# Decode layer on one core: projection, gate and up with the matrix as the moving operand, rows turned by small matmuls, and 128 rows of w_down loaded as 121 and 7

## Chip, cores and metric

One NeuronCore of a Trainium2 chip runs the whole kernel, written in Bass with its waits placed by hand. The metric is the device time of one execution in microseconds (us); the median of three executions of the kernel before is 203.09 us.

## The reference

One token of a decoder layer with cached attention and a gated feed-forward part, all in bf16. There is one row of 640 numbers, 32 heads of 128, 4096 cached positions and 1728 hidden columns:

```python
B, Sq, D = 1, 1, 640
Hq, Hkv, Sk, Dh = 32, 32, 4096, 128
...
q = (x @ wq).reshape(B, Sq, Hq, Dh).transpose(0, 2, 1, 3)
scores = jnp.einsum("bhqd,bhkd->bhqk", q, k) * (Dh ** -0.5)
p = _softmax(scores, axis=-1)
o = jnp.einsum("bhqk,bhkd->bhqd", p, v)
return o.transpose(0, 2, 1, 3).reshape(B, Sq, Hq * Dh) @ wo
...
g = jnp.einsum("bsd,df->bsf", x, w_gate)      # 640 x 1728
u = jnp.einsum("bsd,df->bsf", x, w_up)
h = _gelu(g) * u
return jnp.einsum("bsf,fd->bsd", h, w_down)   # 1728 x 640
...
x = A_x
h = x + _A_ref(_layernorm(x), A_k_cache, A_v_cache, A_wq, A_wo)
h2 = h + _B_ref(_layernorm(h), B_w_gate, B_w_up, B_w_down)
```

The matrices are read once each: the caches are 32 MB each, wq and wo 5 MB each, the three matrices of the feed-forward part 2.2 MB each.

## The kernel before

**Queues.** Every operation is put into a list of its engine by the helpers `V` (VectorE), `A` (ScalarE), `T` (TensorE), `GP` (GpSimd) and `P.dma`. `emit` writes the lists out engine by engine in the order in which they were filled, and `_run` puts a semaphore wait ahead of an operation for what it depends on. All large loads are issued from SyncE's queue (SP) in a fixed order; the issue of a load into a slot waits for the work that frees that slot. The helper `matmul_again` (line 28) is a matmul that uses the weights that are already loaded.

**Attention.** The heads go in eight groups `G` of four. `order` is K0 V0 K1 V1 ... K5 V5 K6 K7 V6 V7; each is a 4 MB load into one of three slots. For a group of K, `score_mult` (L287) multiplies on VectorE, `fold` sums on TensorE, and `score_exp` reduces (L305) and exponentiates (L309) into `p_bd`. For a group of V, `pv_group` multiplies on TensorE with four column tiles side by side into `po`, two PSUM banks. `pick` (L345) keeps the rows that belong together, `pick_sum` (L350) adds them into `po_r`, `p_sum` (L341) sums the exponentials, and `head_sum` (L356) puts the group's heads into place. `scores` runs what `first` and `later` hold, so that the sums of one group are queued among the multiplications of the next.

**Projection.** After four groups `z_sum`, `normalize`, `spread` and `take` leave the heads' output as the columns `aP`. `proj_part` (L386) uses w_o as the stationary operand: each of its 160 matmuls for one half loads a strided 128x128 block and moves one column, so the 640 sums come out as five columns over the partitions, `ps_p`. w_o is loaded in three pieces, `d_wo["0"]`, `["1a"]` and `["1b"]`, into the arena that held wq.

**Feed-forward part.** `h` (L463) adds the input, `layernorm` makes `hlnT`, and `hX` and `resid` (L485) put the residual into the result's bank `ps_d`. `glu` (L476) uses w_gate and then w_up as the stationary operand, 70 matmuls of one column each, into the 14 columns of `ps_g` and `ps_u`. Column m holds the hidden numbers in the order in which w_down's rows lie on the partitions. Operations g1 to g9 (L491 to L499) make `hm`. `down` moves w_down, 160 columns at a time into four column tiles (L506), and four copies and one DMA write the result. The rows 1536 to 1663 of w_down (`wd_sb[:, 12, :]`, 1,280 bytes each) are one load, the first that SP issues after the last V group's matmuls; then come the rows 1664 to 1727, w_gate, w_up in two pieces and the rest of w_down in four pieces.

Of the kernel before, what the change touches and what calls it, by code (L numbers as in the profile page):

```python
# [6 lines left out]
BF16 = mybir.dt.bfloat16  # L7
ALU = mybir.AluOpType
ACTF = mybir.ActivationFunctionType
AX = mybir.AxisListType  # L10

D = 640
# [3 lines left out]
DF = 1728  # L16
# [4 lines left out]
NG = 8  # L21
# [88 lines left out]
def bass_sequential_preLN__gqa_block_cached__glu_gated_geglu__decode_kernel(nc, A_x, A_k_cache, A_v_cache, A_wq, A_wo, B_x, B_w_gate, B_w_up, B_w_down, out):  # L110
# [25 lines left out]
    aP = sb("aP", [128, 2, 16], BF16)  # L136
    sel = sb("sel", [16, 8, 128], BF16)
    g_t = sb("g_t", [128, 14], FP32)
    t1 = sb("t1", [128, 14], FP32)
# [52 lines left out]
    def issue(upto):  # L192
        while state["next"] < min(upto, len(order)):
# [8 lines left out]
                         for i in range(parts)]  # L202
# [20 lines left out]
                                        pattern=[[-1, 4], [-4, 32]], compare_op=ALU.is_equal,  # L223
                                        fill=0.0, base=0, channel_multiplier=1), c_ones)
    c_m8 = GP(lambda e: e.affine_select(m8_t[:, :, :, :], ones_f[:, :].rearrange("p (a b c) -> p a b c", a=8, b=4),
                                        pattern=[[-4, 8], [-32, 4], [-1, 4]], compare_op=ALU.is_equal,
# [8 lines left out]

    c_hs = V(lambda e: e.reduce_sum(hs[:, 12:16], hs_t[:, :, :], axis=AX.X), c_hs, c_hz)
    c_m8 = V(lambda e: e.reduce_sum(m8[:, :], m8_t[:, :, :, :].rearrange("p a b c -> p a (b c)"), axis=AX.X), c_m8)

# [109 lines left out]

    def pick_sum(G):
        evs[G] = V(lambda e: e.reduce_sum(po_r[:, G % 2, :], po_m[:, :, :].rearrange("p b d -> p d b"), axis=AX.X),  # L350
                   mks[G], hds.get(G - 2))
# [30 lines left out]
    def proj_part(t, lo, hi, *ws):  # L382
        def fn(e):
            for c in range(5):
                for i in range(lo, hi):
                    r = e.matmul(ps_p[:, c:c + 1], wo_sb[:, t, i, c::5], aP[:, t, i:i + 1],  # L386
                                 start=(t == 0 and c == 0 and i == 0), stop=(t == 1 and i == 15),
                                 skip_group_check=True)
            return r
        return T(fn, *ws)  # L390
# [3 lines left out]
    def run(todo):  # L394
        while todo:
            todo.pop(0)()

    def scores(G):
        for i in range(4):
            score_mult(4 * G + i)  # L400
            if i >= 1:
                score_exp(4 * G + i - 1)
        run(first)
        score_exp(4 * G + 3)
        run(later)
        issue(pos[("K", G)] + 1 + NSLOT)

    headed = 0
    for kind, G in order:
# [9 lines left out]
        first.append(lambda G=G: pick(G))  # L419
        later += [lambda G=G: pick_sum(G), lambda G=G: p_sum(G)]  # L420
        if G == 4:
            z_sum(0)
            later.append(lambda: normalize(0))
        if G == 5:
# [16 lines left out]
    wd_d = wd_sb[:, 0:12, :].rearrange("p (a r) n -> p a r n", a=3)  # L441
    d_wd = [P.dma("sync", wd_sb[:, 12, :], B_w_down[1536:1664, :], free[1]),
            P.dma("sync", wd_sb[:, 13, 0:320], B_w_down[1664:1728, :].rearrange("f (s n) -> (f s) n", s=2))]
# [5 lines left out]

    V(lambda e: e.memset(ps_g[64:128, 13:14], 0.0), reds[31])  # L450
    V(lambda e: e.memset(ps_u[64:128, 13:14], 0.0), reds[31])
    p_sum(NG - 1)
    pick(NG - 1)
    pick_sum(NG - 1)
    proj_part(0, 0, 16, aPs[0], d_wo["0"])
    z_sum(1)
# [4 lines left out]
    proj_part(1, 0, 12, aPs[1], d_wo["1a"])  # L461
    pr = proj_part(1, 12, 16, d_wo["1b"])
    h = V(lambda e: e.tensor_add(hT[:, 0:5], xx[:, 0:5], ps_p[:, 0:5]), pr)  # L463
    hl = layernorm(hT, h, lambda e: e.tensor_scalar(  # L464
        hlnT[:, :], hT[:, 0:5], ln[:, 0:1], ln[:, 4:5], ALU.subtract, ALU.mult))
# [3 lines left out]

    def glu(ps, w, cs):  # L470
        def fn(e):
            for c in cs:
                for m in range(14):
                    ws = w[:, c, 512 * (m // 4) + m % 4:512 * (m // 4) + 512:4] if m < 12 else \
                        w[:, c, 128 * m:min(128 * m + 128, DF)]
                    i = e.matmul(ps[0:128 if m < 13 else 64, m:m + 1], ws, hlnT[:, c:c + 1],  # L476
                                 start=(c == 0 and m == 0), stop=(c == 4), skip_group_check=True)
            return i
        return fn
    ga = T(glu(ps_g, wg_sb, range(5)), hl, d_wg)  # L480


    def resid(e):
        for q in range(4):
            i = e.matmul(ps_d[32 * q:32 * q + 1, 0:160], ones_f[:, 0:1],  # L485
                         hX[:, 32 * q:32 * q + 32, :].rearrange("p a c -> p (a c)"), start=True, stop=False)
        return i
    T(resid, hx)
    T(glu(ps_u, wu_sb, range(3)), d_wu[0])
    up = T(glu(ps_u, wu_sb, range(3, 5)), d_wu[1])  # L490
    g1 = V(lambda e: e.tensor_copy(g_t[:, :], ps_g[:, 0:14]), ga)  # L491
# [5 lines left out]
    g8 = V(lambda e: e.reciprocal(t1[:, :], t2[:, :]), g7)  # L497
    g6 = V(lambda e: e.tensor_mul(gu[:, :], g_t[:, :], t1[:, :]), g8)
    g9 = V(lambda e: e.tensor_mul(hm[:, :], gu[:, :], ps_u[:, 0:14]), g6, up)  # L499

# [11 lines left out]
    h2 = V(lambda e: e.tensor_mul(hm2[:, :], par[:, :], ps_z[:, 0:1].to_broadcast([128, 2])), hp)  # L512
    T(down([12]), d_wd[0])
    T(down(range(4)), d_wd[2])
# [40 lines left out]
```

## Time and profile before

| what | value |
|---|---|
| median of 3 executions | 203.09 us (203.05 to 203.23) |
| the profiled execution: its time, its span | 203.16 us, 201.9 us |
| busy: PE, PE weight loads, DVE, ACT, POOL | 119.5, 26.2, 128.5, 50.3, 5.5 us |
| instructions | 1934 |
| DMA | 4332 packets, 84.35 MB, mean 418 GB/s |
| instruction packets (queue q8) | 6, 0.10 MB |
| TensorE clock, from 184 us to the end | 0.50 of full speed |

The span is the time from the first to the last instruction in the trace; the execution's own time has 1.26 us more around it. Lines such as L386 are lines of the kernel before. In the windows, the columns are the stretch in us, its length, then busy us and instructions of PE, PEld (weight loads), DVE, ACT and POOL, the clock granted to TensorE, the share of the 16 DMA engines at work, and GB/s. In the timeline, the columns are start, length, engine, line, operation, what it writes and reads, and in brackets the idle time before it and what ended that.

### The profile page before, as it was taken

How to read it: one execution, taken by the hardware profiler on the slowest of the kernel's cores; microseconds unless marked ns; L12 is line 12 of the kernel's file. 1: busy time of each engine (PE TensorE's matmuls, PEld its weight loads, DVE VectorE, ACT ScalarE, POOL GpSimd, SP SyncE). 2: the span in 40 equal slices, each digit the busy share in tenths (PEclk: the TensorE clock that was granted, in tenths of full speed). 3: DMA queues.
4: the chain of work that ended last, by engine and by line, in shares of the span. 5: the costliest groups of instructions: out<-in, count | busy, mean ns of one | idle time of the engine just before them, and what ended most of it. 6: DMA issues, size and time to landing. Idle time of an engine off the chain costs nothing.

```text
span 201.9 us, 1934 instructions
## 1 busy us (share of the span) xinstructions
PE 119.5 (59%) x962; PEld 26.2 (13%) x590; DVE 128.5 (64%) x127; ACT 50.3 (25%) x137; POOL 5.5 (3%) x14
## 2 busy tenths in 40 slices
PE   0108067467843884395559741965397095797595
PEld 0101000010000000000010010001000000176583
DVE  1200189427993799479858966797779978591321
ACT  2100004600550055014502530243025224400101
POOL 7300000000000000000000000000000000000000
PEclk9999999955899589969886997699759979995555
DMA  9999999999999999999999999999999999999992
GB/s 349 422 417 441 441 415 422 428 448 441 438 415 422 422 441 454 430 422 417 428 422 458 428 428 428 422 435 441 435 435 415 412 432 437 414 404 435 412 410 89
DMA packets 4332, 84.35 MB, mean 418 GB/s; under 512 B 482, under 2 KB 868, under 8 KB 1508
## 3 DMA queue, kind: packets, MB, share of 16 engines
q1 hardware_dynamic: 4322, 84.23, 97.7%
q8 instruction: 6, 0.10, 0.2%
q14 instruction: 2, 0.02, 0.0%
q10 hardware_dynamic: 2, 0.00, 0.0%
HBM read 84.23 MB, written 0.00 MB: 417 GB/s over the span
## 4 chain that ended last, share of the span: by engine, by line
DMA 53%; DVE 21%; PE 19%; issue 4%; ACT 2%; SPq 2%
DMA slot<-in_A_k_cache_dram 43%; DVE prod L287 16%; PE bank L28 13%; DMA slot<-in_B_w_down_dram 9%; PE bank L328 3%; DVE sc L305 3%; PE bank L297 2%; ACT p_bd L309 2%; SPq L59 2%; DVE po_r L350 1%; DVE po_m L345 1%; PE bank L506 0%; DVE out_row L519 0%; DVE RT L341 0%; DVE aP L380 0%
## 5 line engine op out<-in xcount | busy, mean ns | idle before, releaser
L287 DVE TENSOR_TENSOR prod<-slot,qb 128x4096 bf16<-128x4096 bf16 x32 | 72.4, 2284 | 24.4 <-DMA slot<-in_A_k_cache_dram 24.4
L309 ACT ACTIVATE p_bd<-sc,zero_t 32x32 bf16<-32x32 f32 x128 | 46.4, 362 | 108.0 <-DVE sc L305 106.8
L28 PE MATMUL bank<-prod,id_b 128*128 128x512 bf16 x224 | 68.0, 455 | 0.0
L297 PE MATMUL bank<-prod,id_b 128*128 128x512 bf16 x32 | 15.4, 482 | 47.2 <-DVE prod L287 47.1
L305 DVE TENSOR_REDUCE sc<-bank 128x32 f32<-128x512 f32 x32 | 22.0, 688 | 15.0 <-PE bank L28 15.0
L328 PE MATMUL bank<-slot,p_bd 128*32 128x512 bf16 x128 | 14.2, 431 | 15.0 <-ACT p_bd L309 13.8
L297 PEld LDWEIGHTS bank<-prod,id_b 128*128 128x128 bf16 x32 | 3.5, 109 | 110.9 <-DVE prod L287 110.9
L350 DVE TENSOR_REDUCE po_r<-po_m 128x128 f32<-128x1024 f32 x8 | 15.2, 1899 | 0.1
L28 PE MATMUL bank<-slot,p_bd 128*32 128x512 bf16 x128 | 14.2, 433 | 0.0
L345 DVE TENSOR_TENSOR po_m<-bank,m 128x1024 f32<-128x1024 f32 x8 | 9.7, 1214 | 1.2 <-PE bank L28 1.2
L328 PEld LDWEIGHTS bank<-slot,p_bd 128*32 128x32 bf16 x128 | 3.7, 104 | 35.3 <-ACT p_bd L309 26.1
L476 PE MATMUL bank<-hlnT,slot 128*128 128x1 bf16 (+1 forms) x140 | 6.7, 176 | 1.7 <-DMA slot<-in_B_w_gate_dram 1.7
L272 PE MATMUL bank<-arena,xlnB 128*32 128x512 bf16 x20 | 3.3, 627 | 7.0 <-DMA arena<-in_A_wq_dram 7.0
L277 DVE CAST qb<-bank 128x512 bf16<-128x512 f32 x1 | 0.7, 692 | 9.9 <-PE bank L28 9.9
L386 PE MATMUL bank<-aP,arena 128*128 128x1 bf16 x160 | 6.7, 178 | 0.3 <-DVE aP L380 0.3
L476 PEld LDWEIGHTS bank<-hlnT,slot 128*128 128x128 bf16 (+1 forms) x140 | 6.3, 118 | 2.6 <-DVE hlnT L464 1.8
L386 PEld LDWEIGHTS bank<-aP,arena 128*128 128x128 bf16 x160 | 6.6, 131 | 0.6 <-DVE aP L380 0.4
L255 ACT ACTIVATE ln<-ln,eps_t 128x1 f32<-128x1 f32 x2 | 0.6, 294 | 20.2 <-DVE ln L253 20.2
L341 DVE TENSOR_REDUCE RT<-p_bd 128x4 f32<-128x512 bf16 x8 | 5.3, 676 | 0.0
L244 PE MATMUL bank<-one_bf,x_row 1*128 1x1 bf16 x5 | 0.4, 178 | 6.8 <-DMA x_row<-in_A_x_dram 6.8
L356 PE MATMUL bank<-po_r,hs 128*16 128x128 f32 x16 | 3.3, 290 | 0.6 <-DVE po_r L350 0.6
L28 PE MATMUL bank<-arena,xlnB 128*32 128x512 bf16 x20 | 3.3, 633 | 0.0
(68 smaller groups left out, 28.9 us busy)
## 6 DMA issues: line engine op xcount, KB each, us to landing
slot<-in_A_k_cache_dram SPq DMA_DIRECT2D x8, 4096.0 KB, 21.3
slot<-in_A_v_cache_dram SPq DMA_DIRECT2D x7, 4096.0 KB, 18.2
arena<-in_A_wq_dram SPq DMA_DIRECT2D x1, 5120.0 KB, 15.1
slot<-in_A_v_cache_dram SPq DMA_DIRECT2D x2, 2048.0 KB, 14.8
arena<-in_A_wo_dram SPq DMA_DIRECT2D x1, 2560.0 KB, 22.7
slot<-in_B_w_gate_dram SPq DMA_DIRECT2D x1, 2160.0 KB, 11.3
arena<-in_A_wo_dram SPq DMA_DIRECT2D x1, 1920.0 KB, 26.9
slot<-in_B_w_up_dram SPq DMA_DIRECT2D x1, 1296.0 KB, 13.9
```

The source lines that it names most:

```text
L28: return e.add_instruction(mybir.InstMatmult(name=nc.get_next_instruction_name(), engine=e.engine, start_tensor_calc=start, stop_tensor_ca ...
L59: ev = self.op(eng, lambda e: e.dma_start(out, in_), *deps, dma=True)
L287: m = V(lambda e: e.tensor_tensor(out=prod[:, s % 4, :, :], in0=kt[:, 32 * u:32 * u + 32, :], in1=qb[:, G, :].unsqueeze(1).to_broadcast([1 ...
L297: i = e.matmul(*args, start=True, stop=False)
L305: reds[s] = V(lambda e: e.reduce_sum(sc[:, s % 4, :], ps_f[s % 2][:, :].rearrange("p (g d) -> p g d", d=16), axis=AX.X), folds[s], exps.ge ...
L309: x = A(lambda e, j=j: e.activation(p_bd[32 * j:32 * j + 32, G % 2, 32 * (s % 4):32 * (s % 4) + 32, j], sc[32 * j:32 * j + 32, s % 4, :], ...
L328: return e.matmul(*args, start=(c < 4), stop=(c >= 12))
L341: sums[G] = V(lambda e: e.reduce_sum(RT[:, 4 * G:4 * G + 4], p_bd[:, G % 2, :, :].rearrange("p g j -> p j g"), axis=AX.X), exps[4 * G + 3])
L345: mks[G] = V(lambda e: e.tensor_tensor(out=po_m[:, :, :], in0=po[:, :].rearrange("p (b d) -> p b d", b=8), in1=m8[:, :].unsqueeze(2).to_br ...
L350: evs[G] = V(lambda e: e.reduce_sum(po_r[:, G % 2, :], po_m[:, :, :].rearrange("p b d -> p d b"), axis=AX.X), mks[G], hds.get(G - 2))
L386: r = e.matmul(ps_p[:, c:c + 1], wo_sb[:, t, i, c::5], aP[:, t, i:i + 1], start=(t == 0 and c == 0 and i == 0), stop=(t == 1 and i == 15), ...
L476: i = e.matmul(ps[0:128 if m < 13 else 64, m:m + 1], ws, hlnT[:, c:c + 1], start=(c == 0 and m == 0), stop=(c == 4), skip_group_check=True)
```

## The change

- `proj_part` makes w_o the moving operand: one column of `aP` is loaded into a column tile and 320 columns of w_o move, in four tiles side by side, into rows 0, 32, 64 and 96 of banks 0 and 1. The four rows are cast to bf16 as a high and a low part (`A_hi`, `A_lo`), and `columns` adds and turns them by ten small matmuls against `ones4` into the five columns of `ps_p`.
- `glu` makes w_gate and w_up the moving operand, 512 columns at a time in four tiles, into rows 0, 32, 64 and 96 of `po`. `turn` casts those rows (gate on VectorE, up on ScalarE) and turns them by six matmuls against `sel4` into the 14 columns.
- `pick_sum` of the last two groups is three additions instead of one reduction. `p_sum` of a group stands at the end of `scores` of the next.
- Rows 1536 to 1663 of w_down are loaded as 121 and 7 rows.
- The constants `sel4` and `ones4` are made at the start; the two memsets of `ps_g` and `ps_u` move behind `h`.

```diff
@@ -135,6 +135,11 @@
     aT = sb("aT", [16, 2, 128], BF16)
     aP = sb("aP", [128, 2, 16], BF16)
     sel = sb("sel", [16, 8, 128], BF16)
+    A_hi = sb("A_hi", [128, D], BF16)
+    A_lo = sb("A_lo", [128, D], BF16)
+    rows = [sb("rows%d" % i, [128, 512], BF16) for i in range(2)]
+    sel4 = sb("sel4", [128, 4], BF16)
+    ones4 = sb("ones4", [128, 1], BF16)
     g_t = sb("g_t", [128, 14], FP32)
     t1 = sb("t1", [128, 14], FP32)
     t2 = sb("t2", [128, 14], FP32)
@@ -222,6 +227,8 @@
     c_hs = GP(lambda e: e.affine_select(hs_t[:, :, :], ones_f[:, :].rearrange("p (a b) -> p a b", a=4),
                                         pattern=[[-1, 4], [-4, 32]], compare_op=ALU.is_equal,
                                         fill=0.0, base=0, channel_multiplier=1), c_ones)
+    c_s4 = GP(lambda e: e.affine_select(sel4[:, :], ones_b[:, 0:4], pattern=[[-32, 4]], compare_op=ALU.is_equal,
+                                        fill=0.0, base=0, channel_multiplier=1), c_onesb)
     c_m8 = GP(lambda e: e.affine_select(m8_t[:, :, :, :], ones_f[:, :].rearrange("p (a b c) -> p a b c", a=8, b=4),
                                         pattern=[[-4, 8], [-32, 4], [-1, 4]], compare_op=ALU.is_equal,
                                         fill=0.0, base=0, channel_multiplier=1), c_ones)
@@ -234,6 +241,7 @@
     c_pbd = GP(lambda e: e.memset(p_bd[:, :, :, :], 0.0))
 
     c_hs = V(lambda e: e.reduce_sum(hs[:, 12:16], hs_t[:, :, :], axis=AX.X), c_hs, c_hz)
+    c_o4 = V(lambda e: e.reduce_max(ones4[:, :], sel4[:, :], axis=AX.X), c_s4)
     c_m8 = V(lambda e: e.reduce_sum(m8[:, :], m8_t[:, :, :, :].rearrange("p a b c -> p a (b c)"), axis=AX.X), c_m8)
 
     V(lambda e: e.reduce_sum(par[:, :], par_t[:, :, :], axis=AX.X), c_par)
@@ -347,6 +355,11 @@
             in1=m8[:, :].unsqueeze(2).to_broadcast([128, 8, DH]), op=ALU.mult), pvs[G], evs.get(G - 1), c_m8)
 
     def pick_sum(G):
+        if G >= NG - 2:
+            a1 = V(lambda e: e.tensor_add(po_m[:, 0:4, :], po_m[:, 0:4, :], po_m[:, 4:8, :]), mks[G])
+            a2 = V(lambda e: e.tensor_add(po_m[:, 0:2, :], po_m[:, 0:2, :], po_m[:, 2:4, :]), a1)
+            evs[G] = V(lambda e: e.tensor_add(po_r[:, G % 2, :], po_m[:, 0, :], po_m[:, 1, :]), a2, hds.get(G - 2))
+            return
         evs[G] = V(lambda e: e.reduce_sum(po_r[:, G % 2, :], po_m[:, :, :].rearrange("p b d -> p d b"), axis=AX.X),
                    mks[G], hds.get(G - 2))
 
@@ -381,11 +394,16 @@
 
     def proj_part(t, lo, hi, *ws):
         def fn(e):
-            for c in range(5):
-                for i in range(lo, hi):
-                    r = e.matmul(ps_p[:, c:c + 1], wo_sb[:, t, i, c::5], aP[:, t, i:i + 1],
-                                 start=(t == 0 and c == 0 and i == 0), stop=(t == 1 and i == 15),
-                                 skip_group_check=True)
+            for i4 in range(lo, hi, 4):
+                for half in range(2):
+                    for i in range(i4, i4 + 4):
+                        a = 32 * (i - i4)
+                        args = (bank[half][a:a + 1, 0:320], aP[:, t, i:i + 1], wo_sb[:, t, i, 320 * half:320 * half + 320])
+                        start, stop = t == 0 and i < 4, t == 1 and i >= 12
+                        if half == 0:
+                            r = e.matmul(*args, start=start, stop=stop)
+                        else:
+                            r = matmul_again(nc, *args, start, stop, (128, 32), (0, a))
             return r
         return T(fn, *ws)
 
@@ -403,6 +421,8 @@
         run(first)
         score_exp(4 * G + 3)
         run(later)
+        if G > 0:
+            p_sum(G - 1)
         issue(pos[("K", G)] + 1 + NSLOT)
 
     headed = 0
@@ -417,7 +437,7 @@
             head_sum(headed)
             headed += 1
         first.append(lambda G=G: pick(G))
-        later += [lambda G=G: pick_sum(G), lambda G=G: p_sum(G)]
+        later.append(lambda G=G: pick_sum(G))
         if G == 4:
             z_sum(0)
             later.append(lambda: normalize(0))
@@ -439,7 +459,8 @@
     wu_v = B_w_up[:, :].rearrange("(p c) n -> p c n", c=5)
     wd_v = B_w_down[0:1536, :].rearrange("(a p r) n -> p a r n", a=3, r=4)
     wd_d = wd_sb[:, 0:12, :].rearrange("p (a r) n -> p a r n", a=3)
-    d_wd = [P.dma("sync", wd_sb[:, 12, :], B_w_down[1536:1664, :], free[1]),
+    d_w12 = [P.dma("sync", wd_sb[lo:hi, 12, :], B_w_down[1536 + lo:1536 + hi, :], free[1]) for lo, hi in ((0, 121), (121, 128))]
+    d_wd = [None,
             P.dma("sync", wd_sb[:, 13, 0:320], B_w_down[1664:1728, :].rearrange("f (s n) -> (f s) n", s=2))]
     d_wg = P.dma("sync", wg_sb, B_w_gate[:, :].rearrange("(p c) n -> p c n", c=5), free[0])
     d_wu = [P.dma("sync", wu_sb[:, 0:3, :], wu_v[:, 0:3, :]),
@@ -447,12 +468,10 @@
     d_wd += [P.dma("sync", wd_d[:, a, lo:hi, :], wd_v[:, a, lo:hi, :])
              for a, lo, hi in ((0, 0, 4), (1, 0, 4), (2, 0, 3), (2, 3, 4))]
 
-    V(lambda e: e.memset(ps_g[64:128, 13:14], 0.0), reds[31])
-    V(lambda e: e.memset(ps_u[64:128, 13:14], 0.0), reds[31])
     p_sum(NG - 1)
     pick(NG - 1)
     pick_sum(NG - 1)
-    proj_part(0, 0, 16, aPs[0], d_wo["0"])
+    proj_part(0, 0, 16, aPs[0], d_wo["0"], reds[4 * NG - 1])
     z_sum(1)
     head_sum(NG - 1)
     normalize(1)
@@ -460,34 +479,62 @@
     take(1)
     proj_part(1, 0, 12, aPs[1], d_wo["1a"])
     pr = proj_part(1, 12, 16, d_wo["1b"])
+    hi = [V(lambda e: e.tensor_copy(A_hi[0:97, 0:320], bank[0][0:97, 0:320]), pr),
+          A(lambda e: e.copy(A_hi[0:97, 320:640], bank[1][0:97, 0:320]), pr)]
+    lo = [V(lambda e, t=t: e.tensor_sub(A_lo[0:97, 320 * t:320 * t + 320], bank[t][0:97, 0:320], A_hi[0:97, 320 * t:320 * t + 320]),
+            hi[t]) for t in range(2)]
+
+    def columns(part, start):
+        def fn(e):
+            for c in range(5):
+                i = e.matmul(ps_p[:, c:c + 1], part[0:97, c::5], ones4[0:97, 0:1], start=(start and c == 0), stop=not start,
+                             skip_group_check=True)
+            return i
+        return fn
+    T(columns(A_hi, True), *hi, c_o4)
+    pr = T(columns(A_lo, False), *lo)
     h = V(lambda e: e.tensor_add(hT[:, 0:5], xx[:, 0:5], ps_p[:, 0:5]), pr)
+    z0 = V(lambda e: e.memset(ps_g[64:128, 13:14], 0.0), lo[0])
+    z1 = V(lambda e: e.memset(ps_u[64:128, 13:14], 0.0), lo[1])
     hl = layernorm(hT, h, lambda e: e.tensor_scalar(
         hlnT[:, :], hT[:, 0:5], ln[:, 0:1], ln[:, 4:5], ALU.subtract, ALU.mult))
     hx = V(lambda e: e.tensor_tensor(out=hX[:, :, :], in0=id_f[:, :].unsqueeze(2).to_broadcast([128, 128, 5]),
                                      in1=hT[:, 0:5].unsqueeze(1).to_broadcast([128, 128, 5]), op=ALU.mult), h, c_idf)
 
 
-    def glu(ps, w, cs):
+    def glu(k, w, cs):
         def fn(e):
             for c in cs:
-                for m in range(14):
-                    ws = w[:, c, 512 * (m // 4) + m % 4:512 * (m // 4) + 512:4] if m < 12 else \
-                        w[:, c, 128 * m:min(128 * m + 128, DF)]
-                    i = e.matmul(ps[0:128 if m < 13 else 64, m:m + 1], ws, hlnT[:, c:c + 1],
-                                 start=(c == 0 and m == 0), stop=(c == 4), skip_group_check=True)
+                for a in range(4):
+                    n = min(512, DF - 512 * a)
+                    i = e.matmul(po[32 * a:32 * a + 1, 512 * k:512 * k + n], hlnT[:, c:c + 1], w[:, c, 512 * a:512 * a + n],
+                                 start=(c == 0), stop=(c == 4))
             return i
         return fn
-    ga = T(glu(ps_g, wg_sb, range(5)), hl, d_wg)
-
+
+    def turn(k, ps, ev, z):
+        cp = (V, A)[k](lambda e: (e.copy if k else e.tensor_copy)(rows[k][0:97, :], po[0:97, 512 * k:512 * k + 512]), ev)
+
+        def fn(e):
+            for r in range(4):
+                i = e.matmul(ps[:, r:12:4], rows[k][0:97, r::4], sel4[0:97, 0:3], start=(r == 0), stop=True, skip_group_check=True)
+            for m in (12, 13):
+                n = 128 if m < 13 else 64
+                i = e.matmul(ps[0:n, m:m + 1], rows[k][0:97, 128 * (m - 12):128 * (m - 12) + n], sel4[0:97, 3:4],
+                             start=False, stop=True, skip_group_check=True)
+            return i
+        return T(fn, cp, z, c_s4)
 
     def resid(e):
         for q in range(4):
             i = e.matmul(ps_d[32 * q:32 * q + 1, 0:160], ones_f[:, 0:1],
                          hX[:, 32 * q:32 * q + 32, :].rearrange("p a c -> p (a c)"), start=True, stop=False)
         return i
+    ga = T(glu(0, wg_sb, range(5)), hl, d_wg, mks[NG - 1])
     T(resid, hx)
-    T(glu(ps_u, wu_sb, range(3)), d_wu[0])
-    up = T(glu(ps_u, wu_sb, range(3, 5)), d_wu[1])
+    ga = turn(0, ps_g, ga, z0)
+    T(glu(1, wu_sb, range(3)), d_wu[0])
+    up = T(glu(1, wu_sb, range(3, 5)), d_wu[1])
     g1 = V(lambda e: e.tensor_copy(g_t[:, :], ps_g[:, 0:14]), ga)
     g2 = V(lambda e: e.tensor_mul(t1[:, :], g_t[:, :], g_t[:, :]), g1)
     g3 = V(lambda e: e.tensor_scalar(t2[:, :], t1[:, :], GELU_C1, 1.0, ALU.mult, ALU.add), g2)
@@ -496,6 +543,7 @@
     g7 = V(lambda e: e.tensor_scalar(t2[:, :], e_t[:, :], 1.0, None, ALU.add), g5)
     g8 = V(lambda e: e.reciprocal(t1[:, :], t2[:, :]), g7)
     g6 = V(lambda e: e.tensor_mul(gu[:, :], g_t[:, :], t1[:, :]), g8)
+    up = turn(1, ps_u, up, z1)
     g9 = V(lambda e: e.tensor_mul(hm[:, :], gu[:, :], ps_u[:, 0:14]), g6, up)
 
     def down(ms, qs=range(4)):
@@ -510,7 +558,7 @@
     hp = T(lambda e: e.matmul(ps_z[:, 0:1], sel2[:, :, :].rearrange("p a b -> p (a b)"), hm[0:64, 13:14],
                               start=True, stop=True), g9, c_sel2)
     h2 = V(lambda e: e.tensor_mul(hm2[:, :], par[:, :], ps_z[:, 0:1].to_broadcast([128, 2])), hp)
-    T(down([12]), d_wd[0])
+    T(down([12]), *d_w12)
     T(down(range(4)), d_wd[2])
     T(down([13]), h2, d_wd[1])
     T(down(range(4, 8)), d_wd[3])
```

## Prediction

> **What bounds the kernel now.** I read the page's slices first, then the chain, then the last microseconds in windows and in the timeline. In the slices, the row DMA is the mean busy share of the 16 DMA engines in tenths:
>
> ```profile
> span 201.9 us, 1934 instructions
> ...
> PEclk9999999955899589969886997699759979995555
> DMA  9999999999999999999999999999999999999992
> ```
>
> The engines are full from the first slice to the last but one: the 84.23 MB are the time. The chain of waits, asked from 174 us on (start, length, what), says the same of the end:
>
> ```profile
> 180.85 18.40 DMA slot<-in_B_w_down_dram
> 199.25 0.04 issue
> 199.30 0.75 PE bank L506 x16
> 200.04 0.30 DVE out_row L519
> ```
>
> Matmuls of `down` wait for the last pieces of w_down, then come two copies and the output's DMA. So the question is when the last DMA engine finishes. The windows (last two columns: DMA share, GB/s) show that they don't finish together:
>
> ```profile
> 196.50:197.00 0.50, 0.50 (x15) 0.49 (x14) 0.00 (x0) 0.00 (x0) 0.00 (x0) 0.50 1.00 394
> ...
> 197.25:197.50 0.25, 0.00 (x1) 0.01 (x1) 0.17 (x1) 0.00 (x0) 0.00 (x0) 0.50 0.59 225
> ...
> 198.00:198.25 0.25, 0.25 (x20) 0.25 (x12) 0.00 (x0) 0.00 (x0) 0.00 (x0) 0.50 0.37 149
> 198.25:198.50 0.25, 0.25 (x17) 0.25 (x9) 0.00 (x0) 0.00 (x0) 0.00 (x0) 0.50 0.28 108
> ...
> 199.00:199.25 0.25, 0.11 (x4) 0.00 (x0) 0.00 (x0) 0.00 (x0) 0.00 (x0) 0.50 0.10 36
> ```
>
> Share times 16 is the number of engines at work: 16, then 9, 6, 4.5, 1.6. In the trace's records the last load's 16 completions come in two clusters: eleven at 197.50 to 198.68, five at 199.11 to 199.66. Following each engine's packets back to back, the five late ones are those that each carried one 16 KB instruction packet (queue q8, at 52.6, 110.0, 174.7, 184.0 and 193.8 us, 0.99 to 1.11 us each).
>
> The work beside that stream stands in the timeline:
>
> ```profile
> 175.58 1.99 DVE L350 TENSOR_REDUCE po_r<-po_m 128x128 f32<-128x1024 f32 x1
> ...
> 183.76 3.36 PE L386 MATMUL bank<-aP,arena 128*128 128x1 bf16 x80 [0.27 <-DVE aP L380]
> 187.15 0.16 DVE L463 TENSOR_TENSOR hT<-xx,bank 128x5 f32<-128x5 f32 x1 [3.45 <-PE bank L386]
> ...
> 189.88 3.35 PE L476 MATMUL bank<-hlnT,slot 128*128 128x1 bf16 x70 [1.71 <-DMA slot<-in_B_w_gate_dram]
> ...
> 197.27 0.17 DVE L499 TENSOR_TENSOR hm<-gu,bank 128x14 bf16<-128x14 f32 x1 [2.17 <-PE bank L476]
> ...
> 197.61 1.50 PE L506 MATMUL bank<-slot,hm 128*1 128x160 bf16 x40
> ```
>
> The gate waits for its load, and `down`'s first 40 matmuls have started all at 198.76 and end at 199.11, 0.14 us before the piece for rows 8 to 10 lands (199.25). Compute is hidden by 0.14 us only, so it has to be costed too.
>
> **The 121 and 7 rows.** 128 rows of 1,280 B are 8 packets on each engine, 52 ns apart (a packet is 55 ns): 0.42 us an engine. No transfer of before has a row count that 16 doesn't divide, save the single row of x, one packet on one engine. Bounds: all 121 rows on one engine, 121 x 0.052 = 6.3 us, 5.9 more than now; or spread over 16, nothing. Every transfer seen gives each engine that it uses the same number; the only equal shares of 121 among up to 16 engines, one aside, are 11 x 11, so I take that, and 7 x 1. Then seven engines carry 12 rows (+0.21 us), four 11 (+0.16), five none (-0.42). No record numbers the engines. If the five are the late ones, the last completion moves from 199.66 to 199.24, above the other eleven (198.68 + 0.21 = 198.89): -0.42.
>
> [...]
>
> SP issues one DMA more, 0.47 us from start to start, so its last load goes out at 181.8 instead of 181.3. The engines work on w_o until 184.0; with that cover gone it would cost 0.47.
>
> **Instruction packets.** Loads and matmuls on PE: projection 320 to 96, gate and up 280 to 80, turning 24, columns 20; 380 fewer. In the trace one packet comes per 217 to 311 PE records. After the one at 174.7 the next then falls near the resid step (about 192 us) and the rest don't come before the end. One late engine ends 1.1 us earlier; that counts only if it is the last one (then the next, 199.57, is last): 0 to 0.09. I take 0.02.
>
> **Up to the residual sum.** pick_sum as three adds: TENSOR_TENSOR takes 0.82 for 640 elements (L466) and 1.22 for 1024 (L345), so 0.69, 0.42 and 0.29 for 512, 256 and 128, 1.46 with gaps, against 1.99. p_sum(6), 0.64, moves into DVE's idle 1.15 us before 174.32. DVE then runs: pick(6) to 175.55, adds to 177.05, p_sum(7) to 177.72, pick(7) to 178.96, adds to 180.45. From head_sum to aP takes 1.70 as now: 182.2; piece 1a of w_o lands at 182.39. Four matmuls side by side start 0.13 us apart for 160 columns at clock 0.5 (L506), so a group of 320 takes 0.27: six groups to 184.05, 1b (landed 184.00) two more, about 184.8, against 187.1. Turning gives that back: cast of 320 columns 0.49 (between L491's 0.17 for 14 elements and L277's 0.69 for 512), two subtractions of 0.49, five small matmuls 0.35 (80 take 3.36): 186.7 for h instead of 187.15. Two memsets (0.06 each) now sit in front of the layernorm. hlnT is ready at about 189.3 instead of 189.6. The gate's load lands at 189.7 (189.3 when relieved): no gain, no cost.
>
> **Gate, up and turning.** A group of four times 512 columns takes 0.43 at clock 0.5 (the PV groups: 0.43 slow, 0.22 fast): gate 5 x 0.43 = 2.1 against 3.35. The cast by DVE takes 0.69 (L277) beside resid's 0.71; then six matmuls, 0.18 + 5 x 0.042 = 0.39. With the start at 189.5 PE reaches up's first part at 192.9 and ends it at 194.2; the second part lands at 194.54 (194.96 now). Then 0.85, 0.1 of drain, ACT's cast 0.59 (L278), 0.39 and three gaps of 0.04: hm at 196.6 instead of 197.27. Bounds of the turn: 0.3 less (clock 1.0) to 1.1 more (copy and matmuls at double). The relieved piece 8-10 lands at 198.83; PE needs 1.84 us from hm to there (199.11 - 197.27), so hm may be as late as 197.0: 0.4 to spare. That cover gone, each us costs one.
>
> **Constants.** One select more on POOL (0.3) and one reduce on DVE (0.29) at 4 to 7 us; p_bd's first writer comes at 31.5. New waits (gate on pick(7), 179.0; projection on the last score reduce, 173.2) are over long before. p_sum's other moves permute 0.64 us on DVE; the K and V loads it could delay are issued 7 to 12 us ahead of their turn. Nothing.
>
> **Sum.** The profiled execution took 203.16 us, 201.9 span and 1.26 around it, 0.07 above the median 203.09. 203.16 - 0.42 - 0.02 = 202.72; against the median, 202.65.
>
> **Rivals.**
> - *The relief misses (0.13).* The late engines are among the eleven that take more. For: nothing in the records says which engines they are. Against: five late and five relieved is a match. The last engine gets +0.16 to +0.21: 203.25 to 203.30. [...]
> - *The turn becomes last (0.17), slower.* Place: between up's second load and hm. If cast and matmuls cost 1.1 more, hm comes at 197.7, 0.7 past the point from which it decides; with half of the relief lost as well (0.2 to 0.4), 203.3 to 203.7, say 203.55. For: four operations in a row where now there is one, and rows that end in PSUM at four partitions. Against: each has a near row above.
> - *No relief (0.13).* The 121 rows spread over all engines. The end stays: 203.1.
> - *One engine takes all 121 rows (0.04).* 5.9 us more on it, from a finish 0 to 2.2 us before the last: 207 to 209.
>
> **How the numbers follow.** The forecast has 0.53; its own range is 202.3 to 202.9 (0.02 to 0.09 of packets, 0.1 of clock and spread, 0.2 of a turn that eats some of it). A difference of 0.2%, 0.41 us, is about what a measurement of this kernel can tell from no change; the forecast sits just beyond. Faster: 0.40 of the 0.53 and 0.02 of no relief, 0.42. Same: 0.13 of the forecast, 0.09 of the miss, 0.11 of no relief, 0.33. Slower: 0.04 + 0.17 + 0.04 = 0.25. Range 202.25 to 203.5: it leaves out the single engine, half of the turn's case and the forecast's tail.
>
> **What would show it.** Right: the shares of the last 2 us fall more steeply, with no run of five engines after the others; the last w_down piece lands near 198.8; hm before 197.0; four or five q8 packets; the gate waits for its load. Wrong: PE or ACT idle on the cast of up's rows just before hm, `down`'s 40 matmuls ending after the piece for 8-10 has landed, or a DMA share of the last us that falls in the same two steps as now.

## Result: 0.46% slower, and the profile after

| | before | after |
|---|---|---|
| median, us | 203.08 (12 runs, 202.85 to 203.39) | 204.12 (12 runs, 203.17 to 204.57) |
| ratio after / before | | 1.0046 [1.0036, 1.0056] |
| profiled execution, us (span) | 203.16 (201.9) | 203.17 (201.9) |

The forecast was 202.65 us in a range of 202.25 to 203.5. The kernel became slower by 1.04 us in the medians, and the median lies above the range. The ratio is taken over all runs and is not the quotient of the two medians, which is 1.0051.

The profiled execution of after is the fastest of its twelve runs, 0.95 us below their median, and as long as the one of before. The loss can't be read from its length, so the unchanged kernel was profiled once more: 204.19 us, span 202.9 (the first experiment). "First trace" and "second trace" below are these two. The page of the first, its slices and queue q8:

```profile
span 201.9 us, 1570 instructions
...
PEclk9999856996996799959997978798569859997575
DMA  9999999999999999999999999999999899999993
...
q8 instruction: 4, 0.07, 0.1%
```

There are 364 instructions fewer and two instruction packets fewer (six before), both close to the forecast. The row DMA differs in two digits: slice 32, 156.5 to 161.5 us, shows 8 instead of 9, and the last slice 3 instead of 2; no step of the prediction turns on the first. The end of the chain of waits (start, length, what), first trace:

```profile
181.28 18.00 DMA slot<-in_B_w_down_dram
199.28 0.04 issue
199.32 0.74 PE bank L554 x15
200.06 0.30 DVE out_row L567
```

and second trace:

```profile
181.37 18.93 DMA slot<-in_B_w_down_dram
200.30 0.04 issue
200.34 0.74 PE bank L554 x14
201.08 0.30 DVE out_row L567
```

Both end as before ended: a piece of w_down, sixteen matmuls, the copies. Only the landing of the piece moves, 199.25 before, 199.28 and 200.30 after. The windows in which before was read (us of the window, then PE, PEld, DVE, ACT, POOL busy, granted clock, DMA share, GB/s), first trace:

```profile
196.50:197.00 0.50, 0.23 (x5) 0.12 (x2) 0.17 (x1) 0.00 (x0) 0.00 (x0) 1.00 0.99 397
197.25:197.50 0.25, 0.25 (x20) 0.23 (x21) 0.16 (x1) 0.00 (x0) 0.00 (x0) 0.90 1.12 446
198.00:198.25 0.25, 0.11 (x8) 0.11 (x12) 0.00 (x0) 0.00 (x0) 0.00 (x0) 0.50 0.91 343
198.25:198.50 0.25, 0.25 (x14) 0.25 (x8) 0.00 (x0) 0.00 (x0) 0.00 (x0) 0.50 0.58 220
199.00:199.25 0.25, 0.00 (x0) 0.00 (x0) 0.00 (x0) 0.00 (x0) 0.00 (x0) 0.50 0.10 36
```

and second trace:

```profile
198.25:198.50 0.25, 0.25 (x16) 0.18 (x8) 0.00 (x0) 0.00 (x0) 0.00 (x0) 0.50 0.67 256
199.00:199.25 0.25, 0.09 (x6) 0.09 (x10) 0.00 (x0) 0.00 (x0) 0.00 (x0) 0.50 0.25 97
199.50:199.75 0.25, 0.25 (x12) 0.02 (x4) 0.00 (x0) 0.00 (x0) 0.00 (x0) 0.50 0.09 36
200.00:200.25 0.25, 0.00 (x0) 0.00 (x0) 0.00 (x0) 0.00 (x0) 0.00 (x0) 0.50 0.06 20
```

In the first trace the engines do end closer together, as the relief of the late ones was to bring about: all 16 at work until 197.5, then a steep fall. But the fall comes 1 us later than before: the share is 0.58 at 198.25 to 198.50, where before had 0.59 at 197.25 to 197.50. In the second trace the fall is as late and one engine goes on alone to 200.7. In both, all 16 engines have more time to spend than before, though the bytes are the same 84.23 MB. Where it is spent shows in the window from 182 to 184 us, in which the two new loads run beside the last of w_o. Before, then the first and the second trace of after:

```profile
182.00:184.00 2.00, 1.23 (x16) 0.66 (x17) 0.52 (x3) 0.00 (x0) 0.00 (x0) 0.50 1.16 461
```
```profile
182.00:184.00 2.00, 0.98 (x24) 0.30 (x12) 0.03 (x1) 0.00 (x0) 0.00 (x0) 0.95 1.22 349
```
```profile
182.00:184.00 2.00, 0.98 (x24) 0.30 (x12) 0.13 (x1) 0.00 (x0) 0.00 (x0) 0.97 1.17 331
```

The engines are as busy (1.16 to 1.22) and move a quarter less: 461 against 349 and 331 GB/s. 2 us x (461 - 349) GB/s is 224 KB, at 417 GB/s 0.54 us; for 331 it is 0.62 us. The packet records give the same: a row of 1,280 B takes 55 ns before, 84 and 87 after.

### The profile page after: what moved, and what is told of

It reads as the page before. It is cut to its first block, busy times and chain, and to the rows that moved or that the text cites. A ratio compares the mean times of both kernels' runs of the same rounds, so it can differ in the third digit from the quotient of the medians.

```text
span 201.9 us, 1570 instructions
## 1 busy us (share of the span) xinstructions
PE 115.4 (57%) x788; PEld 17.1 (8%) x384; DVE 129.6 (64%) x136; ACT 51.3 (25%) x139; POOL 5.6 (3%) x15
## 3 DMA queue, kind: packets, MB, share of 16 engines
q1 hardware_dynamic: 4324, 84.23, 98.1%
HBM read 84.23 MB, written 0.00 MB: 417 GB/s over the span
## 4 chain that ended last, share of the span: by engine, by line
DMA 52%; DVE 21%; PE 19%; issue 3%; ACT 2%; SPq 2%
DMA slot<-in_A_k_cache_dram 43%; DVE prod L295 16%; PE bank L28 13%; DMA slot<-in_B_w_down_dram 9%; DVE sc L313 3%; PE bank L336 3%; PE bank L305 2%; ACT p_bd L317 2%; SPq L59 2%; DVE po_r L363 1%; DVE po_m L353 1%; PE bank L554 0%; DVE out_row L567 0%; DVE RT L349 0%; DVE aP L393 0%
## 5 line engine op out<-in xcount | busy, mean ns | idle before, releaser
L336 PE MATMUL bank<-slot,p_bd 128*32 128x512 bf16 x128 | 14.8, 449 | 15.0 <-ACT p_bd L317 13.8
L28 PE MATMUL bank<-slot,p_bd 128*32 128x512 bf16 x128 | 14.9, 451 | 0.0
L363 DVE TENSOR_REDUCE po_r<-po_m 128x128 f32<-128x1024 f32 x6 | 11.2, 1868 | 0.0
L510 PE MATMUL bank<-slot,hlnT 128*1 128x512 bf16 (+1 forms) x40 | 4.0, 484 | 2.3 <-DMA slot<-in_B_w_gate_dram 1.8
L404 PE MATMUL bank<-arena,aP 128*1 128x320 bf16 x32 | 2.5, 314 | 1.6 <-DMA arena<-in_A_wo_dram 1.6
L286 ACT CAST qb<-bank 128x512 bf16<-128x512 f32 x1 | 0.6, 586 | 10.7 <-PE bank L28 10.7
```

The source lines that it names most:

```text
L28: return e.add_instruction(mybir.InstMatmult(name=nc.get_next_instruction_name(), engine=e.engine, start_tensor_calc=start, stop_tensor_ca ...
L336: return e.matmul(*args, start=(c < 4), stop=(c >= 12))
L510: i = e.matmul(po[32 * a:32 * a + 1, 512 * k:512 * k + n], hlnT[:, c:c + 1], w[:, c, 512 * a:512 * a + n], start=(c == 0), stop=(c == 4))
```

## The experiments

All comparisons are with the kernel before, run beside on the same chip.

**The unchanged kernel once more, for a second trace.**

> The changed kernel once more, for a second trace beside the first, whose execution (203.17 us) was the fastest of its twelve (median 204.12). Theory A, the uneven load: the 121 rows give eleven engines three or four rows more, and in a typical execution the instruction packets fall on some of those eleven and not on the five that were spared; then the typical trace ends about 1 us later than the first one, its last w_down piece lands near 200.6 instead of 199.67, and one engine is late alone. Theory B, the turn: the last w_down piece lands near 199.6 as before, but hm comes after 197.4 and the 40 matmuls of down end after the piece for rows 8 to 10 has landed. Median 203.9 to 204.3 in both.

Measured: median 203.83 (8 runs, 203.22 to 204.19), 1.0027 [1.0014, 1.0040]; the profiled one 204.19. The median is just under the 203.9 to 204.3 that was expected. The piece of w_down for rows 8 to 10 lands 1.02 us later than in the first trace (200.30 against 199.28), the last piece as much later (200.69 against 199.67), and PE waits for both.

**The 128 rows in one load again, all else as after.**

```diff
-    d_w12 = [P.dma("sync", wd_sb[lo:hi, 12, :], B_w_down[1536 + lo:1536 + hi, :], free[1]) for lo, hi in ((0, 121), (121, 128))]
-    d_wd = [None,
+    d_wd = [P.dma("sync", wd_sb[:, 12, :], B_w_down[1536:1664, :], free[1]),
...
-    T(down([12]), *d_w12)
+    T(down([12]), d_wd[0])
```

> The changed kernel with the 128 rows of w_down in one load again, all else as changed. Theory A: the loss is the split's, so this is at or a little under the kernel before, 202.7 to 203.2. Theory B: the loss is the compute's, so this stays at 204.0 to 204.5.

Measured: 203.15 (11 runs, 202.93 to 203.39), 1.0001 [0.9993, 1.0010]. The window of this kernel, called "unsplit" from here on:

```profile
182.00:184.00 2.00, 1.34 (x24) 0.39 (x12) 0.17 (x1) 0.00 (x0) 0.00 (x0) 0.52 1.16 465
```

465 GB/s is no less than the 461 of before. The whole loss goes with the split, and the rest of the change is worth nothing that can be measured.

**The split alone, in the kernel before** (the same three lines, the other way).

> The kernel before with the 121 and 7 rows alone. Theory A: the loss comes with it, 203.8 to 204.4. Theory B: no loss, 202.7 to 203.3.

Measured: 204.07 (5 runs, 203.90 to 204.25), 1.0050 [1.0038, 1.0062]; its window:

```profile
182.00:184.00 2.00, 1.65 (x40) 1.57 (x41) 0.20 (x2) 0.00 (x0) 0.00 (x0) 0.50 1.09 318
```

318 GB/s with the old compute. So the split by itself makes the whole loss.

**112 and 16 rows, then 64 and 64.** The changed kernel with these counts, all of them multiples of 16. That all 16 engines then get equal shares is the author's estimate, from the loads of before, where 128 rows are 8 packets on each of 16 engines; no record names a packet's engine.

```diff
-    ... for lo, hi in ((0, 121), (121, 128))]
+    ... for lo, hi in ((0, 112), (112, 128))]     # and, in the other kernel, ((0, 64), (64, 128))
```

> [...] Theory A1, uneven counts: what costs is that some engines carry more rows than others; then this is as the kernel with one load, 203.0 to 203.3, and its 1,280-byte packets take 55 ns. Theory A2, the paths into SBUF: what costs is that the engines' rows no longer lie where each engine writes alone, so that packets of all engines slow down while the load is in flight (in the traces with 121 rows: 79 to 87 ns instead of 55 for 1,280 bytes, 290 instead of 200 for 5,120, between 182 and 184 us); then packets take 70 to 90 ns here too, the mean completion of the last load comes 0.3 to 0.8 us later than 198.46, and the time is 203.4 to 203.9.

> The same with 64 and 64 rows: 4 and 4 on each of 16 engines, even again. Theory A1: 203.0 to 203.3, packets of 55 ns. Theory A2: half of the partitions are written by all engines at a time; packets of 1,280 bytes take about twice 55 ns, the mean completion of the last load comes 0.4 to 1.0 us later than 198.46, the time is 203.5 to 204.1. [...]

Measured: 203.65 (5 runs), 1.0033 [1.0020, 1.0046], and 203.83 (5 runs), 1.0038 [1.0024, 1.0051]. If the shares are equal, as estimated, equal shares don't take the loss away, and uneven ones aren't its main part. The 1,280-byte packets took 68 and 72 ns: between the 55 of the single load and the 84 to 87 of 121 and 7, and far from twice 55.

**Two loads of all 128 rows, each half of the columns.**

```diff
-    ... for lo, hi in ((0, 121), (121, 128))]
+    d_w12 = [P.dma("sync", wd_sb[:, 12, lo:hi], B_w_down[1536:1664, lo:hi], free[1]) for lo, hi in ((0, 320), (320, 640))]
```

> The changed kernel with the 128 rows as two loads again, but cut by columns: twice 128 rows of 320 columns (640 bytes). It has the second DMA, its issue on SP and its completions like the split by rows, but every load has 128 rows on 16 engines. Theory A2 (the split by rows slows all packets because engines no longer write apart): packets between 182 and 184 us keep 55, 32 and 200 ns, the mean completion of the last load stays at 198.4 to 198.6 (at most 0.1 more for smaller packets), the time is 203.0 to 203.3. If instead two loads in place of one are what costs, it is 203.6 or more.

Measured: 203.08 (11 runs), 0.9996 [0.9987, 1.0005]. One more load, one more issue by SP and packets of half the size cost nothing that shows (203.08 against 203.10 for before beside it). It is the rows.

**The same rows to other partitions.** Two loads of 64 rows each, the same 64 rows of w_down, once into the slice of `wd_sb` and once into an unused stretch of the other slot; the other 64 rows aren't loaded. If the partitions that are written make the slowing, the two kernels differ; if the reading of HBM or a load of fewer than 128 rows as such makes it, both are as slow as 64 and 64 (203.83). Number and size of the packets are the same in both kernels; the partitions differ, 32 to 95 or 0 to 63. The rows that are read differ with them, 1568 to 1631 or 1536 to 1599, but the single load of 128 rows reads both at 55 ns a packet.

```diff
-    ... for lo, hi in ((0, 121), (121, 128))]
+    d_w12 = [P.dma("sync", dst, B_w_down[1536 + lo:1600 + lo, :], free[1])
+             for dst in (wd_sb[lo:lo + 64, 12, :], sl[1][lo:lo + 64, 14 * D:15 * D])]     # lo = 32, or lo = 0
```

> The changed kernel with two loads of 64 rows (the bytes and counts of 64 and 64), but both go to partitions 32 to 95, the second into an unused stretch of the same partitions; 64 of the 128 rows are loaded twice and the others not at all. Rows, sizes, queue and the rows of HBM that one engine reads are those of a load of 64 rows; only the partitions differ from the partner run. [...]

> The partner: both loads of 64 rows go to partitions 0 to 63; again 64 rows are loaded twice and the others not at all. [...]

Measured: 203.04 (11 runs), 0.9998 [0.9989, 1.0007], for partitions 32 to 95, and 204.34 (5 runs), 1.0058 [1.0046, 1.0071], for 0 to 63. The windows, in this order:

```profile
182.00:184.00 2.00, 1.06 (x28) 0.30 (x12) 0.17 (x1) 0.00 (x0) 0.00 (x0) 1.00 1.16 465
```
```profile
182.00:184.00 2.00, 0.99 (x24) 0.31 (x12) 0.13 (x1) 0.00 (x0) 0.00 (x0) 1.00 1.17 289
```

465 against 289 GB/s, and 1.3 us in the time, from the choice of partitions. Loads of 64 rows as such aren't slow (203.04). The slow one is slower than 64 and 64, of which only one load goes to partitions 0 to 63 (204.34 against 203.83). Why 0 to 63 are slower than 32 to 95 isn't shown.

The packet records (means over the packets that start from 182 to 184 us) and the sixteen completions of the last load, for all of these kernels:

| rows of the loads | 1,280 B packet, ns | 5,120 B packet (w_o), ns | last load's completions: mean, last, us | median, us |
|---|---|---|---|---|
| 128 (before) | 55 | 200 | 198.46, 199.66 | 203.08 |
| 128 (unsplit) | 55 | 200 | 198.46, 199.85 | 203.15 |
| 128, by columns | none | 200 | 198.39, 199.47 | 203.08 |
| 64 twice, partitions 32 to 95 | 55 | 200 | 198.41, 199.71 | 203.04 |
| 112, 16 | 68 | 257 | 199.04, 200.14 | 203.65 |
| 64, 64 | 72 | 279 | 199.15, 200.31 | 203.83 |
| 121, 7 (first trace) | 84 | 295 | 199.08, 199.67 | 204.12 |
| 121, 7 (second trace) | 87 | 294 | 199.17, 200.69 | 203.83 |
| 121, 7 (split alone) | 79 | 289 | 199.26, 200.53 | 204.07 |
| 64 twice, partitions 0 to 63 | 83 | 342 | 199.62, 200.76 | 204.34 |

The third column is the one to read: the 5,120-byte packets of w_o, another load's, are slowed about as much, in proportion, as the split's own rows. The mean completion says what each engine loses on average: nothing in the upper four, 0.6 to 1.2 us in the lower six.

**One engine with 0.77 us more.** In the unsplit kernel a 20 KB load into one partition, ahead of the others. It isolates what an uneven share costs without the row split.

```diff
+    d_ex = P.dma("sync", slots[1][0:1, 0:16 * D], B_w_down[0:16, :].rearrange("a n -> (a n)").unsqueeze(0), free[1], consumed[13])
...
-    P.op("sync", None, d_out)
+    P.op("sync", None, d_out, d_ex)
```

> The changed kernel with one load of 128 rows, and an additional load of 20 KB into a single partition (data that nothing uses) queued in front of it, as one packet or few on one engine, 0.77 us at the 26.6 bytes per ns of the 32 KB packets. It tells what uneven load costs by itself. The last load's 16 completions spread over 2.2 us and the engines that carried an instruction packet come last: if the additional load falls on one of those, the end comes up to 0.77 us later; if not, it is hidden. So executions of two kinds, 203.0 to 203.3 and 203.6 to 204.0, more of the first; packets of other engines keep 55 and 200 ns. If the load is cut over 16 engines, nothing changes beyond 0.05.

Measured: 203.12 (11 runs, 202.89 to 203.40), 0.9998 [0.9989, 1.0007]. The load is one packet of 773 ns on one engine, and it is hidden in every run; the second group that was expected, 203.6 to 204.0, did not come. The engine that it fell on had that much room.

**w_up's loads left out, in before and in the unsplit kernel.** Up is computed from w_gate's data. This takes 2.2 MB out of the stream, so that the compute comes to light. The edit is shown for the unsplit kernel; in before it is the same with `ps_u` in place of 1.

```diff
-    d_wu = [P.dma("sync", wu_sb[:, 0:3, :], ...), P.dma("sync", wu_sb[:, 3:5, :], ...)]
...
-    T(glu(1, wu_sb, range(3)), d_wu[0])
-    up = T(glu(1, wu_sb, range(3, 5)), d_wu[1])
+    T(glu(1, wg_sb, range(3)), d_wg)
+    up = T(glu(1, wg_sb, range(3, 5)), d_wg)
```

> The kernel before without the two loads of w_up (2.2 MB, about 5.2 us at 420 GB/s); up is computed from w_gate's data instead, so that all operations stay and only the load is left out. With it the loads end at about 194.4 us and the operations behind the gate are what ends last: gate at 189.9, hm at 197.3 as now, then 56 matmuls of down in 2.0, the copies and the output: 202.6 to 203.0, that is 0.1 to 0.5 below the kernel before.

> The changed kernel with one load of 128 rows and without the loads of w_up, as a partner to the run above. If the new projection, gate and up are really shorter and only hidden behind the loads, this is 0.9 to 1.5 us faster than its partner (gate 2.1 instead of 3.35, up 2.1 instead of 3.4, given back 1.1 for up's turn): 201.3 to 201.9. If they are not shorter, both are the same within 0.3.

Measured: 202.77 (10 runs), 0.9986 [0.9977, 0.9995], and 200.80 (4 runs, 200.28 to 202.38), 0.9902 [0.9867, 0.9937]. The chain of waits of before without w_up:

```profile
193.76 3.31 PE bank L474 x70
...
197.17 0.18 DVE hm L497
...
197.58 2.00 PE bank L504 x56
```

and of the unsplit kernel without w_up:

```profile
193.16 1.26 PE bank L507 x5
...
194.44 0.59 ACT rows L513
...
195.63 0.18 DVE hm L544
...
196.04 1.11 PE bank L551 x56
```

Now both chains run over compute. The new one is 2.0 us shorter in the medians: up with its turn takes 2.5 us (193.16 to 195.63) where the old up took 3.4 (193.76 to 197.17), and the 56 matmuls of `down` take 1.11 instead of 2.00, at a granted clock of 1.00 instead of 0.50. The compute part of the change is thus a real gain, hidden by the loads. It was more than the expectation allowed (0.9 to 1.5 us), which had no term for the clock. The profiled run of the new kernel is the fastest of its four, 200.28, 200.49, 201.10 and 202.38 us; the slowest of them has the lowest mean clock, 0.817 against 0.846 to 0.859. So the size of the gain differs from run to run.

**One copy of four partitions at the end**, in the unsplit kernel, as a version that might beat both: one VectorE copy of 97 partitions, and the output written from four of them.

```diff
-    dn = {q: T(down([11], [q]), d_wd[5]) for q in (0, 2, 1, 3)}
+    dn = T(down([11]), d_wd[5])
...
-    os = [V(... out_row[0:1, 160 * q:160 * q + 160], ps_d[32 * q:32 * q + 1, 0:160] ...) for q in range(2)]   # and two by ACT
-    d_out = P.dma("sync", out[0, :, :], out_row[:, :], *os)
+    os = V(lambda e: e.tensor_copy(out4[0:97, :], ps_d[0:97, 0:160]), dn)
+    d_out = P.dma("sync", out[0, :, :].rearrange("a (q n) -> (a q) n", q=4), out4[0:97:32, :], os)
```

> The changed kernel with one load of 128 rows, and the result's four rows copied by one instruction of VectorE over partitions 0 to 96 instead of two each on VectorE and ScalarE, and written from four partitions. Since the end is the last w_down piece plus what follows it, and the two copies one after the other take 0.66 us against 0.31 for one, this should be 0.3 us faster than with two copies: 202.75 to 202.95, unless the output's DMA from four partitions takes longer than from one.

Measured: 203.33 (11 runs, 203.19 to 203.72), 1.0011 [1.0002, 1.0020]. It missed. Its last lines in the timeline (start, length, engine, line, operation):

```profile
199.99 0.33 DVE L567 CAST out<-bank 97x160 bf16<-97x160 f32 x1 [2.65 <-PE bank L554]
200.34 0.62 SPq L59 DMA_DIRECT2D out_dram<-out  x1
```

The copy takes 0.33 instead of 0.66, but SP's issue takes 0.62 where the unsplit kernel has 0.31, and the output lands some 1.6 us after the issue starts against 1.1. None of the runs that load all the data beats before.

## Why the prediction was wrong

The steps of the compute stand in the timeline of the first trace:

```profile
175.71 0.69 DVE L359 TENSOR_TENSOR po_m<-po_m 128x512 f32<-128x512 f32 x1
176.44 0.43 DVE L360 TENSOR_TENSOR po_m<-po_m 128x256 f32<-128x256 f32 x1
176.90 0.29 DVE L361 TENSOR_TENSOR po_r<-po_m 128x128 f32<-128x128 f32 x1
...
181.86 0.17 DVE L393 CAST aP<-bank 128x16 bf16<-128x16 f32 x1 [0.45 <-PE bank L388]
...
184.43 0.43 PE L404 MATMUL bank<-arena,aP 128*1 128x320 bf16 x4 [1.07 <-DMA arena<-in_A_wo_dram]
...
187.04 0.16 DVE L496 TENSOR_TENSOR hT<-xx,bank 128x5 f32<-128x5 f32 x1 [0.45 <-PE bank L490]
...
189.87 1.87 PE L510 MATMUL bank<-slot,hlnT 128*1 128x512 bf16 x17 [1.82 <-DMA slot<-in_B_w_gate_dram]
...
192.22 0.69 DVE L516 CAST rows<-bank 97x512 bf16<-97x512 f32 x1 [2.01 <-PE bank L510]
...
194.99 0.60 PE L510 MATMUL bank<-slot,hlnT 128*1 128x512 bf16 x8 [0.50 <-DMA slot<-in_B_w_up_dram]
195.65 0.59 ACT L516 CAST rows<-bank 97x512 bf16<-97x512 f32 x1 [1.03 <-PE bank L510]
...
196.83 0.17 DVE L547 TENSOR_TENSOR hm<-gu,bank 128x14 bf16<-128x14 f32 x1 [1.52 <-PE bank L523]
```

- **Up to h: right but for the load.** The three adds take 0.69, 0.43 and 0.29 (0.69, 0.42, 0.29 forecast), aP is there at 182.03 (182.2). h starts 0.11 before its old time, not 0.45 earlier: the last piece of w_o, on which the projection waits, is held up by the split and its last completion comes at 184.38 instead of 184.00. The matmuls start at 184.43, and from there 2.61 us to h.
- **Gate and up: close, in part by luck.** hlnT at 189.49 (189.3), the gate at 189.87 (189.5), waiting for its load as said; the casts 0.69 and 0.59 as said. hm starts at 196.83 (196.6). Two differences cancel in part. Up's last eight matmuls start 0.45 later than forecast (194.99 against 194.54), for their load was not relieved. From there to hm it takes 1.84 instead of 2.05, at a granted clock of 1.00 from 194.5 to 197.0, where the forecast assumed 0.50. In the unsplit trace, with 0.50 in that stretch, the same eight matmuls take 1.02 instead of 0.60, start 0.19 later (195.18), and hm starts at 197.46: 2.28 us, so at the assumed clock the step was 0.2 short.
- **Who is last: right as to compute.** At 197.47 in the second trace, where up's second load lands late, hm is 0.5 past the forecast's limit of 197.0, and `down` still ends on a load:

```profile
197.47 0.17 DVE L547 TENSOR_TENSOR hm<-gu,bank 128x14 bf16<-128x14 f32 x1 [1.52 <-PE bank L523]
...
199.16 0.70 PE L554 MATMUL bank<-slot,hm 128*1 128x160 bf16 x16 [0.38 <-DMA slot<-in_B_w_down_dram]
...
200.34 0.70 PE L554 MATMUL bank<-slot,hm 128*1 128x160 bf16 x16 [0.48 <-DMA slot<-in_B_w_down_dram]
```

  The brackets name what ended PE's idle time: two loads. The rival in which the turn becomes last isn't seen in any trace.
- **Instruction packets: right, and worth nothing.** Four, the next one after 174.1 at 194.0 (about 192). The unsplit kernel also has four and isn't faster. What still counts is the engine on which a packet falls, as the second trace shows below.
- **The 121 and 7 rows: the step that failed.** It counted rows on each engine and multiplied by the 52 to 55 ns of before. The counts were right: in the first trace eleven engines complete the first load (182.97 to 184.37 us) and seven the second (183.24 to 184.56), and the loads' queue q1 has 4324 packets against 4322, for the 4-byte packets that end the engines' shares are 11 and 7 in place of 16. The duration was not: 84 to 87 ns, and the packets of w_o beside them went from 200 to 295. The term was sized -0.42; the mean engine got +0.62 and +0.71 (199.08 and 199.17 against 198.46), the last one +0.01 and +1.03 (199.67 and 200.69 against 199.66), and the median, against the unsplit kernel, +0.97. The step asked which engine carries a row and never to which partitions the rows go.
- **The five late engines are the five relieved: right in some executions only.** In the first trace, going by the completions, the engines with an instruction packet all lie among those without rows of the 121. There the relief comes and cancels the slower packets: the mean completion is 0.62 later, the last one at 199.67 as before. In the second trace the engine that is last from the split load to w_up's second piece (195.58) is one that took 12 rows; it ends at 200.28, 0.62 after the last one of before. It is overtaken by an engine on which the instruction packet of 194.12 to 195.14 falls, and which ends at 200.69. (Each engine's share of a load ends with a 4-byte packet: before has 481 of them in q1, 16 for each of 30 loads and one for the output. The last engine's, for rows 0 to 3, starts at 197.03. A usual share of eight packets takes 1.57 us, but no 4-byte packet starts near 195.46; the one that fits starts at 194.10, just ahead of the instruction packet.) Which engines carry the instruction packets differs between executions. Of the 20 times of this kernel four lie at 203.17 to 203.30 and sixteen at 203.73 to 204.57, which would fit the two cases; this was only read from two traces.
- **The rival that the relief misses** had the sign but priced it by counts too, at 203.25 to 203.30; the median came out 0.8 above. That some engines are left out isn't the main part either: 112 and 16 rows, and 64 and 64, which by the author's estimate use all 16, lose 0.33% and 0.38%.

What is shown: the split of the rows makes the loss, by slower packets, those of another load too, while its loads are in flight (5,120-byte packets from 200 ns to between 289 and 295 with 121 and 7 rows); two loads as such, one more issue (203.08) and an uneven share on one engine (203.12) don't; and with equal counts, the choice of partitions switches the slowing on or off (packets of 83 or 55 ns). What is inferred: that the 121 and 7 rows are slow for the same reason. They show the same signs, but in them the partitions and the number of engines change together, and the records name neither a packet's partition nor its engine. So the reason that theory A2 gives, engines that no longer write apart, isn't shown. Open as well: how much of the 0.47 us between the medians of 121 and 7 (204.12) and of 112 and 16 (203.65) is uneven counts and how much is slower packets (84 and 87 ns against 68), and why instruction packets move from engine to engine.

## What to carry to other kernels

In a kernel that is bound by its stream of loads, price a transfer by what it does to the others in flight (here 5,120-byte packets of another load, from 200 ns to between 289 and 295), and ask to which partitions it writes (203.04 for 32 to 95, 204.34 for 0 to 63) as well as on which engines it runs. When a load must be cut, cut its columns and keep all 128 partitions: the two loads of columns took 203.08, the three cuts of its rows 203.65 to 204.12. An engine that is last in one trace may not be last in the next execution (the last completion came at 199.67 and at 200.69), so don't tune the shares of engines by one trace. And when the profiled execution is the fastest of its runs, take another trace before explaining the time.

## What was not expected of the hardware

- A load of 160 KB in two parts slows a load of other data by up to 0.7 of its packets' time: 5,120-byte packets from 200 ns to 257 to 342 while 112 and 16, 64 and 64, 121 and 7, or twice the same 64 rows on partitions 0 to 63, are in flight.
- One engine carried 0.77 us more than its fellows without any change in the time (203.12 against 203.10 for before beside it).
- The granted clock of TensorE differs between executions of the same matmuls: from 194.5 to 197.0 us it was 1.00 in both traces of after and 0.50 in the unsplit one. With w_up left out, the 56 matmuls of `down` ran at 1.00 (1.11 us) behind matmuls that move 512 columns and at 0.50 (2.00 us) behind those that move one; that the form of the matmuls makes this difference is not shown, for the unsplit trace has the 512-column form and 0.50.
- An output of 1,280 B written from four partitions costs SP 0.62 us for the issue, from one partition 0.31.
